# One query unit by way of DRAM, its neighbours spaced anew, and gate stores on GpSimd, in a fused attention and mixture kernel

## The chip, the cores and the metric

The kernel runs on one core of a Trainium2 chip. The engines are named as in the profile: PE (TensorE) multiplies matrices, PEld is its weight load, DVE (VectorE) and ACT (ScalarE) do elementwise work, POOL (GpSimd) does slower elementwise work, SP issues DMAs. The metric is the device time of one execution in microseconds (us); lower is better.

## The reference

Two blocks follow each other. The first is a linear attention with a product feature map, for 4 batches, 4 heads, 1088 tokens and head width 32; the second is a mixture of 4 experts over the 4352 tokens with gates normalised per token, each expert 128 to 1024 to 128.

```python
def phi(x):                                   # S1, S2: 8 x 32
    a = np.einsum('rd,bhsd->bhsr', S1, x)
    b = np.einsum('rd,bhsd->bhsr', S2, x)
    return np.einsum('bhsi,bhsj->bhsij', a, b).reshape(*x.shape[:-1], r * r)
q_p, k_p = phi(q), phi(k)
kv, z = np.einsum('bhsf,bhsd->bhfd', k_p, v), np.sum(k_p, axis=2)
num = np.einsum('bhsf,bhfd->bhsd', q_p, kv)
den = np.einsum('bhsf,bhf->bhs', q_p, z)[..., None] + 1e-06
x = (num / den).transpose(0, 2, 1, 3).reshape(4352, 128)

p = domain_probs / (domain_probs.sum(-1, keepdims=True) + 1e-09)
for e in range(4):
    out += p[:, e:e + 1] * (np.maximum(x @ w1[e], 0.0) @ w2[e])
```

## The kernel before

**The mixture sets the frame.** The tokens are cut into eleven chunks: 128, 448, six of 512, 320, 256 and 128, in the order of the batches. A chunk goes through 16 steps (4 experts, 4 steps each, two blocks of 128 hidden values per step). A half step is one such block: `first` issues its first-layer matmuls, `third` and `lower` finish it, and `behind` issues second-layer matmuls of earlier steps. Chunk 0 and chunk 10 are plain float32 (line 243 in the profile, through `on_side`). Chunk 1 is float32 for experts 0 and 1 (lines 1084 and 1195). All the rest is split into two or three float32r parts: lines 1097, 1098 and 1146 are the first layer, 1214 the second. The splitting of the weights (`weight_parts`, `second_weight_parts`; ACT line 880, DVE line 883) is done at fixed steps during chunks 0 to 2. `ev`, `gate` and `total` (POOL lines 1253 and 1255) weight and sum the experts; `gate` tiles are loaded from the DRAM tensor `gates`, which `store_gates` fills from `pt`.

**The attention is slipped in between.** `start` does the keys of batch 0, its first 128 queries and the projection of the second query unit before chunk 0. What is left is a list, `plan`, of small pieces: (estimated DVE cost, function, name, wait). Each half step of the mixture calls `work`, which adds to a credit, `rate * rooms[...]`, capped at 0.9, and runs pieces while the credit lasts. The rate is what chunks still need over the room that is left until a little ahead of each chunk's start (`EARLY` half steps). A wait such as `("qturn", 2)` holds a piece back until two half steps after the piece of that name. `until_there` forces pieces when a chunk starts. The order so made is fixed when the program is built: each engine then works through its own list in order, and waits where an input is not there.

**Query units.** A batch is cut into three units (`UNITS`). There are two ways for one:

- *Direct* (`queries`, batch 0): transpose the queries (`qT`, line 566), project them on PE with `sq` (line 842), then on DVE two sums and shuffles (lines 845 to 856) lay out both factors, and four half products (line 579) follow.
- *By way of DRAM* (`unit_turn`, `unit_project`, `unit_product`, `unit_visit`; batches 1 to 3): transpose; project on PE with `sx`; ACT copies to `qs` (line 755); SP stores `qs` to `qd` (line 757) and loads it back with repeated rows as `qp` and `qb` (lines 762, 763); DVE makes two full products (line 769).

A *visit* is the PE work against `kvx`, the summed keys of the batch. `attend_inverse`, `attend_scale` and `attend_out` then make the unit's `x` on DVE (`rc`, `xs`, `y`; lines 669 to 695). The second unit of batch 0 is copied by ACT and POOL into the tile `ring` (line 707), from which chunk 1 reads; later units go through the DRAM tensor `xd` into `ring` (lines 713, 722).

**Keys of batches 1 to 3** are 13 pieces each (`key_pieces`: three turns, three projections on line 425 each with its sum, four products), then `key_end` (sums over the tokens on PE, `kvx` on DVE). `load_batch` loads keys and values through SP.

**The lists around the change.** SP's list has, after the weights, 16 gate stores (line 336), two gate loads, then `kn` and `vn` of batch 1. POOL makes `sx` in `later_weights` (line 1014), called at step 8. `sr` is a constant that only `start` reads.

Of the kernel before, what the change touches and what calls it, by code (L numbers as in the profile page):

```python
# [24 lines left out]
def kernel(  # L25
# [30 lines left out]
    R = 8  # L56
# [7 lines left out]
    CW = 512  # L64
    GE = 160
    LA = 2
    LAND, EARLY = 6, 11

    THREE = (0, 1, 3, 4, 5, 6)
    OTHER = [b for b in range(FB) if b not in THREE]  # L70
# [128 lines left out]
        load_w2(e, 1)  # L199
    sk = cpool.tile([P, P], F32, name="sk")  # L200
    sp = apool.tile([32, 3, 2, 32], F32, tag="qf", name="sp")
    sr = cpool.tile([P, 3, 2, P], F32, name="sr")
    sq = cpool.tile([P, P], F32, name="sq")
    sx = cpool.tile([P, P], F32, name="sx")
    nc.gpsimd.memset(sk[:, :], 0.0)
# [122 lines left out]
            out=_ap(pn, 0, P, 0, [[E, G], [1, E]]), in0=dp[:, :, :], in1=_ap(dsum, 0, P, 0, [[1, G], [0, E]]), op=ALU.mult  # L328
        )

    def store_gates():
        nc.vector.transpose(pt[:, :], pn[:, :])
        for b in range(B):
            for e in range(E):
                p = list(pt.ap)[0][0]
                nc.sync.dma_start(
                    gates[b, e].rearrange("(x r j) -> r x j", r=32 // E, j=32),
                    bass.AP(pt.tensor, pt.offset + (32 * b + e) * p, [[E * p, 32 // E], [32, GE // 32], [1, 32]]),
                )
# [178 lines left out]
            for x in range(2):  # L518
                add(0.76, lambda p=p, x=x: key_product(b, 0, NT, p, x, nc.vector), "products")

    def key_end(b, then=None):

        kv = []

        def sums():
            kv.append(held(psum(ps_h, "h")))
            for p in range(2):
                key_sum(b, p, kv[0])
            if then:
                then()  # L530

        def blocked():
            key_blocks(b, kv[0])
            free()

        add(0.1, sums, "keysum", ("products", 3))
        add(0.29, blocked, "keyblocks", ("keysum", 1))
# [31 lines left out]
    def query_turn(b, c, n):  # L569
        qT = apool.tile([P, QW], F32, tag="qT", name="qT")  # L570
        for _ in query_turns(b, c, n, qT):
            pass
        return qT
# [153 lines left out]

    qd = dram.tile([B, len(UNITS[0]), HP, QW], F32, name="qd")

    later = [(b, sum(UNITS[b][:u]), n, u) for b in range(1, B) for u, n in enumerate(UNITS[b])]  # L730
    turned, factors, products, over = {}, {}, {}, {}

    def unit_turn(w):
# [6 lines left out]
    def unit_project(w):  # L740

        b, c, n, u = later[w]
        qT, n2 = turned.pop(w), n // 2
        qc = psum(ps_h, "h")
        for i in range(2):
            for _ in range(2):
                on_side(
                    lambda s: qc[half[s], 0:n2],
                    lambda s: sx[:, HP * i : HP * i + HP],
                    lambda s: qT[:, n2 * s : n2 * s + n2],  # L750
                    start=(i == 0),
                    stop=(i == 1),
                )
        qs = apool.tile([P, QW // 2], F32, tag="qf", name="qs")
        nc.scalar.copy(qs[:, 0:n2], qc[:, 0:n2])
        for s in range(2):
            nc.sync.dma_start(qd[b, u, :, n2 * s : n2 * s + n2], qs[half[s], 0:n2])
        qp = query_tiles()
        qb = [apool.tile([P, QW], F32, tag=t, name="qb") for t in ("qb", "qa")]
        row, at = list(qd[b, u, :, 0:n].ap)[0][0], qd[b, u, :, 0:n].offset  # L760
        for p in range(2):
            nc.sync.dma_start(qp[p][:, 0:n], bass.AP(qd.tensor, at + 16 * p * row, [[row, 16], [0, R], [1, n]]))
            nc.sync.dma_start(qb[p][:, 0:n], bass.AP(qd.tensor, at + (32 + 16 * p) * row, [[0, R], [row, 16], [1, n]]))
        factors[w] = qp, qb

    def unit_product(w, p):
# [15 lines left out]
    def vector_us(n):  # L782

        return 0.16 + n * 1.04e-3
# [3 lines left out]
    def add(cost, run, name, after=None):  # L788

        plan.append((cost, run, name, after))  # L790

    def lay_plan():

        of_first = chain(*(queries(0, c, n) for c, n in ((P, UNITS[0][1]), (P + UNITS[0][1], UNITS[0][2]))))
        for at in range(38):
            add(0.55, lambda: next(of_first, None), "first")
        covers[:] = [(18, P + UNITS[0][1]), (38, S)]
        add(0, lambda: load_rows(q, 1, "qn"), "load")
        key_pieces(1)
        add(vector_us(later[0][2]), lambda: unit_turn(0), "qturn")  # L800
        key_end(1, lambda: unit_project(0))
        for w, (b, c, n, u) in enumerate(later):
            now_on, plan[:] = list(plan), []
            if b + 1 < B:
                if u == 0:
                    key_pieces(b + 1)
                    fill, plan[:] = list(plan), []
                if u == 2:
                    plan[:] = fill
                    key_end(b + 1)  # L810
                else:
                    plan[:], fill = fill[: 5 + u], fill[5 + u :]
            lapse = ("visit" if w else "keysum", LAND)
            for p in range(2):
                add(vector_us(n), lambda w=w, p=p: unit_product(w, p), "product", lapse)
            more = w + 1 < len(later)
            if more:
                add(vector_us(later[w + 1][2]), lambda w=w: unit_turn(w + 1), "qturn")

            def visit(w=w, more=more):  # L820
                if more:
                    unit_project(w + 1)
                unit_visit(w)

            add(0.1, visit, "visit", ("qturn" if more else "product", 2))
            add(0.4, lambda w=w: inverse.__setitem__(w, attend_inverse(*products[w])), "inverse", ("visit", 1))
            add(vector_us(n), lambda w=w: over.__setitem__(w, attend_scale(*products[w], inverse.pop(w))), "scale")
            add(vector_us(n), lambda w=w: unit_out(w), "out")
            plan[:0] = now_on
            covers.append((len(plan), S * b + c + n))  # L830

    covers, inverse = [], {}

    def queries(b, c, n):
        qc = early.pop((b, c), None)
        if qc is None:
            qT = query_turn(b, c, n)
            yield
            yield
            yield  # L840
            qc = held(psum(ps_h, "h"))
            nc.tensor.matmul(qc[:, 0:n], sq[:, :], qT[:, 0:n], start=True, stop=True)
            yield
        qf = apool.tile([P, QW], F32, tag="qf", name="qf")
        nc.vector.stream_shuffle(in_=qc[:, 0:n], out=qf[:, 0:n], mask=mask_lo)
        yield
        nc.vector.tensor_tensor(out=qf[:, 0:n], in0=qc[:, 0:n], in1=qf[:, 0:n], op=ALU.add)
        free()
        yield
        qb = apool.tile([P, QW], F32, tag="qb", name="qb")  # L850
        nc.vector.stream_shuffle(in_=qf[:, 0:n], out=qb[:, 0:n], mask=mask_b)
        yield
        qp = query_tiles()
        for x in range(2):
            qa = apool.tile([P, QW], F32, tag="qa", name="qa")
            nc.vector.stream_shuffle(in_=qf[:, 0:n], out=qa[:, 0:n], mask=mask_a[x])
            yield
            for p in range(2):
                query_product(qp, p, x, n, qa, qb)
                yield  # L860
        yield
        yield
        yield
        yield from attend(b, c, n, qp)
# [142 lines left out]

    def later_weights():

        for h in range(H):
            for to, step, at in ((16 * (h // 2) + h % 2, 2, 0), (32 + R * h, 1, R)):
                nc.gpsimd.tensor_copy(
                    _ap(sx, 32 * h, 32, to, [[HP, 2], [step, R]]), _ap(s_T, 0, 32, at, [[D, 2], [1, R]])
                )
        for h in range(2):
            nc.gpsimd.memset(_ap(by8, 0, P, 32 * h, [[16, 2], [1, 8]]), 1.0 - h)
            nc.gpsimd.memset(_ap(by8, 0, P, 32 * h + 8, [[16, 2], [1, 8]]), 0.0 + h)
        nc.vector.transpose(own8[:, :], by8[:, :])  # L1020
# [246 lines left out]

    start()
    lay_plan()
    place, now, at_of, credit, spent = [0], [0], {}, [0.0], [0.0]  # L1270

    def piece(forced=False):

# [87 lines left out]
    for i in range(len(steps) + LA):  # L1361
        if i < len(steps):
# [11 lines left out]
            def work():  # L1374

                now[0] += 1
                if not NQ <= i < NQ + 2:
                    credit[0] = min(credit[0] + rate * rooms[min(now[0], len(rooms) - 1)], 0.9)
                if holds[0]:
                    credit[0] = max(credit[0], 0.01)  # L1380
                while credit[0] > 0:
                    cost = piece()
                    credit[0] -= cost
                    if not cost:
                        break
# [7 lines left out]
            if i == 2:  # L1393
                gate_quotients()
            elif i == 8:
                later_weights()
            elif i == 5:
                store_gates()
                load_gates(1, range(2))
                load_batch(1)  # L1400
            if m == NC - 2 and kq == NQ // 2:
                until_there(B * S)
                load_last()
# [36 lines left out]
```

## Time and profile before

| | us |
|---|---|
| median of 3 runs | 466.45 (464.6 to 466.86) |
| profiled execution | 466.47 |
| its span, first to last instruction | 464.7 |

| engine | busy us | share of the span |
|---|---|---|
| PE | 452.1 | 97% |
| DVE | 362.5 | 78% |
| ACT | 328.4 | 71% |
| POOL | 110.7 | 24% |

The mean granted clock of PE is 0.996. Chunk 0's matmuls begin at 13.65 us, chunk 1's at 34.85, chunk 1's expert 2 at 62.53, chunk 2 at 84.50, chunk 3 at 138.51.

How to read what follows: a *window* row has the stretch in us from the span's start, its length, the busy us (and instructions) of PE, PEld, DVE, ACT and POOL, the granted clock of PE (1.00 is full), the share of time of the DMA engines and GB/s. A *timeline* row has start, duration, engine, line, operation, out<-in, shape and count; brackets hold the engine's idle time just before and what ended it. The *chain* follows the program back from its last instruction. Matmuls overlap, so a row's duration is longer than the distance to the next one.

### The profile page before, as it was taken

The page shows a single profiled execution, that of the slowest core. Times are in us where ns is not written, and L with a number is a line of the kernel's source. Part 1 is how long each engine was busy: PE and PEld are TensorE (multiplying, and loading weights), DVE is VectorE, ACT ScalarE, POOL GpSimd, SP SyncE. Part 2 cuts the span into 40 slices and gives each one's busy share as a digit, 9 for nine tenths or more (in the row PEclk, how much of TensorE's full clock was granted, in tenths as well). Part 3 has the DMA queues.
Part 4 walks back from the last instruction along what each step waited for, and adds up shares of the span by engine and source line. Part 5 has one row for each costly group of instructions (what it writes and reads, how often), then busy time and mean ns, then how long its engine had stood idle before and what let it go on. Part 6 is the DMA issues. An engine that isn't in the chain of part 4 may idle for free.

```text
span 464.7 us, 8563 instructions
## 1 busy us (share of the span) xinstructions
PE 452.1 (97%) x2991; PEld 350.9 (76%) x2991; DVE 362.5 (78%) x607; ACT 328.4 (71%) x694; POOL 110.7 (24%) x178
## 2 busy tenths in 40 slices
PE   8979999998999999999999999999999999999997
PEld 5765567776777777777777777777777778999987
DVE  5966859798697779787798787787888787878753
ACT  4256568687686678877887776777877786888841
POOL 6320111321332103321233122211221122333120
PEclk9989999999999999999999999999999999999999
DMA  7915060151363314115200340432213210211830
GB/s 221 286 31 129 15 196 20 35 121 37 87 146 119 83 40 108 24 34 137 63 19 27 75 102 14 99 60 86 55 25 99 61 38 16 54 47 31 249 100 18
DMA packets 53171, 37.27 MB, mean 80 GB/s; under 512 B 27304, under 2 KB 47624, under 8 KB 53128
## 3 DMA queue, kind: packets, MB, share of 16 engines
q1 hardware_dynamic: 53112, 36.73, 30.5%
q8 instruction: 23, 0.38, 0.3%
q14 instruction: 20, 0.16, 0.1%
q10 hardware_dynamic: 16, 0.00, 0.0%
HBM read 31.63 MB, written 5.08 MB: 79 GB/s over the span
## 4 chain that ended last, share of the span: by engine, by line
PE 81%; DVE 11%; ACT 3%; DMA 2%; issue 2%; SPq 0%; DVEq 0%; ACTq 0%
PE o L1214 34%; PE h L1146 11%; PE h L1097 10%; PE h L1098 10%; PE h L243 7%; DVE hb L1123 2%; PE o L243 2%; PE h L1084 2%; DVE hd L1126 2%; PE o L1195 2%; PE h L425 1%; DMA kn<-in_k_dram 1%; DMA xd<-y 1%; DVE qp L579 1%; DVE kp L441 1%
## 5 line engine op out<-in xcount | busy, mean ns | idle before, releaser
L1099 ACT ACTIVATE h<-h 128x512 f32<-128x512 f32 (+3 forms) x272 | 146.9, 540 | 80.0 <-PE h L1098 73.8
L1123 DVE SCALAR_TENSOR_TENSOR hb<-h,ha 128x512 fp32r<-128x512 f32 (+3 forms) x204 | 125.8, 625 | 55.8 <-ACT ha L1149 53.8
L1097 PE MATMUL h<-xa,wa 128*128 128x512 f32 (+3 forms) x272 | 125.2, 460 | 0.0
L1126 DVE SCALAR_TENSOR_TENSOR hd<-ha,hb 128x1024 fp32r<-128x1024 f32 (+3 forms) x102 | 117.2, 1149 | 8.5 <-PE h L1098 0.5
L1149 ACT ACTIVATE ha<-h 128x512 fp32r<-128x512 f32 (+3 forms) x204 | 111.7, 547 | 0.0
L1146 PE MATMUL h<-xd,wd 128*128 128x512 f32 (+3 forms) x272 | 103.1, 379 | 0.9 <-ACT h L1099 0.7
L1098 PE MATMUL h<-xb,wb 128*128 128x512 f32 (+3 forms) x272 | 100.4, 369 | 0.0
L1253 POOL TENSOR_TENSOR ev<-ev,gate 128x256 f32<-128x256 f32 (+2 forms) x51 | 41.3, 810 | 233.2 <-DVE ev L1246 213.7
L1214 PE MATMUL o<-ha,vab 128*128 128x512 f32 (+3 forms) x204 | 76.8, 378 | 0.0
L1097 PEld LDWEIGHTS h<-xa,wa 128*128 128x128 f32 x272 | 51.3, 189 | 20.0 <-issue 11.7
L1098 PEld LDWEIGHTS h<-xb,wb 128*128 128x128 f32 x272 | 51.4, 189 | 19.8 <-issue 12.5
L1214 PE MATMUL o<-hid,w_sb 128*128 128x512 f32 (+3 forms) x136 | 63.2, 546 | 0.4 <-DVE ev L1246 0.4
L1146 PEld LDWEIGHTS h<-xd,wd 128*128 128x128 f32 x272 | 51.1, 188 | 13.2 <-ACT h L1099 3.3
L1214 PE MATMUL o<-hd,vd 128*128 128x512 f32 (+3 forms) x204 | 58.9, 370 | 0.0
L1214 PE MATMUL o<-hb,vb 128*128 128x512 f32 (+3 forms) x136 | 50.5, 372 | 0.0
L1255 POOL TENSOR_TENSOR total<-total,ev 128x256 f32<-128x256 f32 (+2 forms) x51 | 45.1, 884 | 4.0
L1214 PEld LDWEIGHTS o<-ha,vab 128*128 128x128 f32 x204 | 38.5, 189 | 6.9 <-issue 0.3
L1214 PEld LDWEIGHTS o<-hd,vd 128*128 128x128 f32 x204 | 36.9, 188 | 6.1
L1154 ACT ACTIVATE hid<-h 128x512 f32<-128x512 f32 (+3 forms) x68 | 37.6, 553 | 0.2 <-PE h L1146 0.2
L1253 POOL TENSOR_TENSOR total<-ev,gate 128x256 f32<-128x256 f32 (+2 forms) x17 | 11.7, 705 | 88.1 <-issue 40.0
L1214 PEld LDWEIGHTS o<-hb,vb 128*128 128x128 f32 x136 | 25.5, 188 | 4.3 <-issue 0.4
L1214 PEld LDWEIGHTS o<-hid,w_sb 128*128 128x128 f32 x136 | 24.5, 188 | 5.1 <-DVE ev L1246 1.0
(142 smaller groups left out, 462.1 us busy)
## 6 DMA issues: line engine op xcount, KB each, us to landing
gate<-gates SPq DMA_DIRECT2D x16, 256.0 KB
kn<-in_k_dram SPq DMA_DIRECT2D x4, 544.0 KB
vn<-in_v_dram SPq DMA_DIRECT2D x16, 128.0 KB
w_sb<-in_moe_w_dram SPq DMA_DIRECT2D x4, 512.0 KB
w_last<-in_moe_w_dram SPq DMA_DIRECT2D x4, 512.0 KB
gate<-gates SPq DMA_DIRECT2D x8, 224.0 KB
qn<-in_q_dram SPq DMA_DIRECT2D x2, 544.0 KB
w_sb<-in_moe_w_dram SPq DMA_DIRECT2D x4, 256.0 KB
```

The costliest lines, as they stand in the source:

```text
L243: nc.tensor.matmul(out(s), weights(s), moving(s), **flags)
L1097: nc.tensor.matmul(g, wa[:, e, w], xa, start=True, stop=False)
L1098: nc.tensor.matmul(g, wb[:, e, w], xb, start=False, stop=True)
L1099: nc.scalar.activation(g, g, ACTF.Copy, scale=1.0 + R12)
L1123: nc.vector.scalar_tensor_tensor(out=hb, in0=g, scalar=0.0, in1=high, op0=ALU.max, op1=ALU.subtract)
L1126: nc.vector.scalar_tensor_tensor(out=d2, in0=a2.bitcast(F32), scalar=R12, in1=b2.bitcast(F32), op0=ALU.mult, op1=ALU.subtract)
L1146: nc.tensor.matmul(g, w, x, start=False, stop=True, skip_group_check=True)
L1149: nc.scalar.activation(ha, g, ACTF.Relu, scale=NEAR)
L1154: nc.scalar.activation(hid[i][j], g, ACTF.Relu)
L1214: nc.tensor.matmul(acc[m, e][o][:, 0:n], w, h, start=first_one, stop=last)
L1253: nc.gpsimd.tensor_tensor(out=to[:, x], in0=ev[:, x], in1=g[:, x], op=ALU.mult)
L1255: nc.gpsimd.tensor_tensor(out=total[m][:, x], in0=total[m][:, x], in1=ev[:, x], op=ALU.add)
```

## The change

- The third unit of batch 0 (512 tokens) goes by way of DRAM like later units. For it a second projection matrix, `first_sx`, is built by POOL in the space of `sr`, with another order of the features, and `qb` is loaded in four pieces per head pair instead of one.
- The pieces get other costs, an order per unit written out by hand (`keys[...]` slices), other waits (products and visits by their own names), the query turn ahead of the products, `EARLY` 14 instead of 11, and a credit cap of 0.5 instead of 0.9.
- `store_gates` is called per batch: batch 0 at step 5 through SP as before, batches 1 to 3 at steps 12, 13 and 14, issued by POOL. So SP's list has 4 gate stores ahead of the gate loads and of `kn` of batch 1, where it had 16.

```diff
-    LAND, EARLY = 6, 11
+    LAND, EARLY = 6, 14
...
-    sr = cpool.tile([P, 3, 2, P], F32, name="sr")
+    sr = cpool.tile([P, 3, 2, P], F32, tag="sr", name="sr")
...
-    def store_gates():
-        nc.vector.transpose(pt[:, :], pn[:, :])
-        for b in range(B):
+    def store_gates(batches):
+        for b in batches:
+            if b == 0:
+                nc.vector.transpose(pt[:, :], pn[:, :])
             for e in range(E):
-                nc.sync.dma_start(
+                (nc.gpsimd if b else nc.sync).dma_start(
...
-    later = [(b, sum(UNITS[b][:u]), n, u) for b in range(1, B) for u, n in enumerate(UNITS[b])]
+    later = [(b, sum(UNITS[b][:u]), n, u) for b in range(B) for u, n in enumerate(UNITS[b]) if b or u == 2]
+    first_sx = {}
...
-                    lambda s: sx[:, HP * i : HP * i + HP],
+                    lambda s: (sx if b else first_sx[0])[:, HP * i : HP * i + HP],
...
+            if b:
+                nc.sync.dma_start(qb[p][:, 0:n], ...)
+                continue
+            for x in range(4):
+                nc.sync.dma_start(
+                    qb[p][32 * x : 32 * x + 32, 0:n],
+                    bass.AP(qd.tensor, at + (32 + 16 * p + R * (x % 2)) * row, [[0, 4], [row, R], [1, n]]),
+                )
...
-        of_first = chain(*(queries(0, c, n) for c, n in ((P, UNITS[0][1]), (P + UNITS[0][1], UNITS[0][2]))))
-        for at in range(38):
-            add(0.55, lambda: next(of_first, None), "first")
-        covers[:] = [(18, P + UNITS[0][1]), (38, S)]
-        add(0, lambda: load_rows(q, 1, "qn"), "load")
-        key_pieces(1)
+        of_first = queries(0, P, UNITS[0][1])
+        costs = [0.62] * 9 + [0.05] * 4 + [0.4, 0.55, 0.6, 0.1, 0.1]
+        for at, cost in enumerate(costs):
+            add(cost, lambda: next(of_first, None), f"first{at}", ("first8", 5) if at == 12 else ("first12", 2) if at == 13 else None)
+        covers.append((len(plan), P + UNITS[0][1]))
         add(vector_us(later[0][2]), lambda: unit_turn(0), "qturn")
-        key_end(1, lambda: unit_project(0))
+        add(0.1, lambda: unit_project(0), "visit", ("qturn", 5))
+        add(0, lambda: None, "wait", ("start", 2 * NQ + 2))
...
+            if b == 0:
+                plan.extend(keys[1][:3])
+            else:
+                at = {(1, 0): (1, 3, 13), (1, 1): (2, 0, 3), (1, 2): (2, 3, 5), (2, 0): (2, 5, 13)}
+                at.update({(2, 1): (3, 0, 3), (2, 2): (3, 3, 9), (3, 0): (3, 9, 13)})
+                if (b, u) in at:
+                    k, z0, z1 = at[b, u]
+                    plan.extend(keys[k][z0:z1])
                 if u == 0:
-                    key_pieces(b + 1)
...
-            lapse = ("visit" if w else "keysum", LAND)
-            for p in range(2):
-                add(vector_us(n), lambda w=w, p=p: unit_product(w, p), "product", lapse)
             more = w + 1 < len(later)
             if more:
                 add(vector_us(later[w + 1][2]), lambda w=w: unit_turn(w + 1), "qturn")
+            for p in range(2):
+                add(vector_us(n), lambda w=w, p=p: unit_product(w, p), "product", ("visit", LAND if w else LAND + 3))
...
-            add(0.1, visit, "visit", ("qturn" if more else "product", 2))
+            add(0.1, visit, "visit", ("product", 3 if w < 4 else 2))
...
-
+        first_sx[0] = cpool.tile([P, P], F32, tag="sr", name="sx0")
+        nc.gpsimd.memset(first_sx[0][:, :], 0.0)
         for h in range(H):
-            for to, step, at in ((16 * (h // 2) + h % 2, 2, 0), (32 + R * h, 1, R)):
+            nc.gpsimd.tensor_copy(
+                _ap(first_sx[0], 32 * h, 32, 16 * (h // 2) + 4 * (h % 2), [[HP, 2], [R, 2], [1, 4]]),
+                _ap(s_T, 0, 32, 0, [[D, 2], [4, 2], [1, 4]]),
+            )
+            for t, to, step, at in (
+                (first_sx[0], 32 + R * h, 1, R), (sx, 16 * (h // 2) + h % 2, 2, 0), (sx, 32 + R * h, 1, R)
+            ):
...
-                    credit[0] = min(credit[0] + rate * rooms[min(now[0], len(rooms) - 1)], 0.9)
+                    credit[0] = min(credit[0] + rate * rooms[min(now[0], len(rooms) - 1)], 0.5)
...
-                store_gates()
+                store_gates(range(1))
                 load_gates(1, range(2))
                 load_batch(1)
+            elif 12 <= i < 12 + B - 1:
+                store_gates(range(i - 11, i - 10))
```

## The prediction

> **What bounds the kernel now.** I read the page's busy table and chain first, then busy time by stage, then the timeline wherever TensorE (PE) was not full. The execution profiled took 466.47 us, its span 464.7, so 1.8 lies outside; the runs' median is 466.45, and sums below start from 466.47.
>
> ```profile
> PE 452.1 (97%) x2991; PEld 350.9 (76%) x2991; DVE 362.5 (78%) x607; ACT 328.4 (71%) x694; POOL 110.7 (24%) x178
> PE 81%; DVE 11%; ACT 3%; DMA 2%; issue 2%; SPq 0%; DVEq 0%; ACTq 0%
> 176.63 3.81 DMA xd<-y
> 170.00:180.00 10.00, 10.00 (x41) 7.48 (x40) 7.34 (x13) 7.15 (x14) 3.77 (x4) 1.00 0.47 116
> ```
>
> The first two lines are the page's busy line and chain: PE is the bound nearly everywhere. The third, from the chain in order of time, looks like a 3.8 us wait for DRAM; the fourth (the window 170 to 180: its length, then busy us of PE, PEld, DVE, ACT, POOL, the granted clock, DMA share, GB/s) shows PE full through it. Nothing is won there. What can be won is where PE stands still or is clocked down.
>
> ```profile
> 3.69:7.11 3.42, 2.13 (x42) 1.40 (x41) 1.97 (x7) 1.37 (x5) 1.49 (x6) 1.00 1.03 238
> 24.17:27.59 3.42, 3.10 (x58) 2.86 (x54) 2.05 (x5) 2.57 (x10) 1.94 (x6) 1.00 0.07 11
> 27.59:31.00 3.41, 1.20 (x4) 0.45 (x6) 1.92 (x5) 1.61 (x5) 0.62 (x3) 1.00 0.05 8
> 31.00:34.41 3.41, 3.41 (x34) 3.41 (x34) 3.00 (x7) 0.38 (x1) 0.00 (x0) 0.50 0.14 37
> 62.53:84.50 21.97, 20.74 (x89) 16.01 (x87) 18.73 (x28) 18.00 (x39) 6.65 (x7) 1.00 0.27 75
> 341.85:353.30 11.45, 11.45 (x72) 8.51 (x72) 9.60 (x13) 8.09 (x16) 2.90 (x4) 1.00 0.10 24
> ```
>
> The same columns. The last row is one expert of a 512-token chunk with nothing else in it: 11.45 us, the floor. In 27.59 to 31.00 PE is busy 1.20 of 3.41 us, and the next stretch of equal length has half the clock.
>
> ```profile
> 26.66 0.61 PE L243 MATMUL h<-x_first,w_sb 128*64 128x128 f32 x8
> 29.80 1.13 PE L842 MATMUL h<-qT,sq 128*128 128x512 f32 x2 [2.53 <-DVE qT L566]
> ...
> 34.85 1.40 PE L1084 MATMUL h<-ring,w_sb 128*128 128x448 f32 x3
> ...
> 48.71 0.69 PE L243 MATMUL h<-kvx,qp 128*64 128x66 f32 x16 [0.88 <-DVE qp L579]
> ...
> 114.53 0.76 PE L243 MATMUL h<-qT,sx 128*64 128x160 f32 x8 [1.25 <-DVE qT L566]
> ```
>
> The timeline of PE, bracketed: idle before, and who ended it. Three stalls: 2.53 us before the third unit's projection, 0.88 before its second head pair, 1.25 before the projection of a later unit.
>
> ```profile
> 24.71 0.67 DVE L695 STREAM_TRANSPOSE y<-xs 128x512 f32<-128x512 f32 x1
> 25.42 2.34 ACT L707 COPY ring<-y 32x128 f32<-32x128 f32 x8 [0.28 <-DVE y L695]
> 19.45 2.03 POOL L1014 COPY sx<-s_T 32x16 f32<-32x16 f32 x8
> 25.45 2.85 POOL L707 COPY ring<-y 32x128 f32<-32x128 f32 x8 [3.65 <-DVE y L695]
> 21.69 11.03 SPq L336 DMA_DIRECT2D gates<-pt x16
> 89.99 1.15 SPq L757 DMA_DIRECT2D qd<-qs  x2
> 92.68 0.58 SPq L762 DMA_DIRECT2D qp<-qd  x1
> ```
>
> Timelines of DVE, ACT, POOL and SP. The 2.34 us of copies into ring stand on ACT ahead of a weight split (27.77) that DVE waits for ahead of that qT. A gate store costs SP 11.03/16 = 0.69 us; from two qd stores to a load of what they wrote it is 2.69 us.
>
> **Part by part. A: chunk 0 and the third unit.** The L842 projection leaves; in the changed order the same unit's projection (four 64x256 matmuls, about 0.95 us) stands behind the last first-layer group of chunk 0, just ahead of chunk 1. The second unit's visit (1.1 us) comes six groups later. PE: from 17.08 thirteen groups at 0.437 us (their pitch in the trace) reach the visit at 22.8, where before it came after seven and waited 0.41. DVE's factors, now behind the 0.9 us of gate sums, are done near 21.9: no wait. Ten groups more: 28.3.
> DVE decides the next point. POOL now makes two matrices: from 19.0 a memset of 0.20 (as for sx), sixteen copies of 0.254 (2.03/8), four small memsets, to 23.5. DVE's own8 transpose waits for that (1.7 us later than before), and behind it stand one split 0.65, one end sum 0.3, a split 0.65, the inverse 0.5, the scaling 0.8, a split 0.65, y 0.67: y ends at 27.7. qT follows at 28.3, when PE asks for it. The projection and one group take PE to 29.7. The ring copies end at 27.7 + 2.85 = 30.55, and chunk 1 starts at 30.6 instead of 34.85: -4.2. PE's idle time near there is some 1 us, so its busy share stays above the 62% (2.13 of 3.42) that kept the full clock, and well above the 35% that did not; 1.7 us (half of 3.41) of the gain is the clock.
> The Trainium skill's page "TensorE: Matmul & The Clock Gate", section "Why this matters for your kernels", asks for no idle gap over about 3 us and tells of a return to half clock after one idle window. By that alone the 2.53 us gap would not have cost the clock, and A would be 1.7 smaller, the total 463.0; the trace has the half clock, so the trace decides.
> Against that: POOL now issues gate stores. Four (batch 1) stand ahead of its ring copies, from 23.5; eight more behind them. Free time is 27.7 - 23.5 = 4.2 us, 1.04 a store. No row shows a store issued by POOL: between 0.12 (its smallest memset) and 2.1 (SP's issue plus half the 2.69 round trip and more, if POOL were held until landing). I take 1.2, SP's 0.69 times 0.73/0.42 (a 128x256 product on POOL against DVE): 4 x 0.16 = +0.6. **A = -3.6**, from -4.2 to +1.7.
>
> **B: the third unit's factors.** Four shuffles (0.73), a sum (0.68) and four half products (0.69) leave DVE, 6.4 us; two full products of 0.68 come in. SP: four stores to 24.5, then gate loads, keys near 27 (33.73 before), values, queries after qT, two qd stores at 31.1, and ten loads of 0.6 from 33.8 to 39.8, landed by 43 if landing takes 3 (kn's first took 4.2). DVE comes to the products near 44.5 and PE to the visit near 50: cover 4 to 5 us, then one for one. The 0.88 us stall goes: **-0.9** (0 if that cover is gone). The later gate stores are wanted past 90 us; keys, nearer, are now loaded 6 us sooner: no cost.
>
> **C: chunk 1's last two experts.** 62.53 to 84.50 is 21.97 us against 2 x 11.45 x 448/512 = 20.0. The key projections of batch 1 (2.1 us of PE) move in here from ahead of it, the next unit's projection (0.95) moves out: PE's sum is unchanged, and is no cost. But ACT, busy 18.00 of 21.97, gets three fs copies and two vx copies, 2.2 us; DVE gets 1.0 and gives back 1.4 (a key product, a qT). Bounds -0.5 and +2.2 (all exposed); **+0.6**, as ACT has 4 us free.
>
> **D: units spaced anew.** Before, qT is the last thing issued ahead of the visit that needs it, two half steps later (a half step is 11.45/8 = 1.43 us). Now it stands ahead of the products, and visits wait three half steps behind those for the early units: the 1.25 us stall at 114.53 goes. **-1.25** (0 if DVE, whose load per expert stays at 9 to 11 of 11.45 us, is late anyway).
>
> **E: due sooner, less saved-up credit.** From 84.5 to 191.8 eight experts cost 8 x 11.45 = 91.6, the attention's own PE pieces 12.5 and switches between matmul kinds about 1.6, together 105.7 of 107.3; D is most of the rest. So sooner due times win nothing: **0**, +-1.
>
> Sum: -3.6 - 0.9 + 0.6 - 1.25 = -5.15, so 461.3.
>
> **Rivals.** (1) POOL holds chunk 1. A store costs 2.1: the ring copies start 4 x (2.1 - 1.04) = 4.2 late, the PE gap passes 4 us, the clock halves (1.7): A = +1.7, 466.6. For it: nothing but the copies feeds ring there. Against: a round trip is a landing time, which SP itself does not wait for between stores.
> (2) Slower: the same place, DVE and POOL getting in each other's way. In the trace a 896-wide hd takes 1.57 us beside a POOL product against 1.09 alone, and a POOL sum 1.46 against 0.74. If each store has to wait out DVE instructions (0.65 each) three times or more, it costs over 2.65, and the total passes 468.8; at 3.5 it is 4 x 2.46 + 1.7 = +11.5 against the -4.2, so 466.47 + 7.3 - 1.55 = 472.2. Against: many DVE instructions there read PSUM or a single tile.
> The Trainium skill's page "SBUF — State Buffer", section "SBUF: two separate sides", gives this rule: DMAs issued by GpSimd need descriptors written by its cores, which DVE instructions in certain modes lock out; it advises the SP or ACT queue. No run here shows it yet.
> (3) The gain is given back in C and the expert behind it: ACT's 2.2 us exposed in both, and D's stall reappearing at an earlier visit: +1.6 + 1.25, about 464.2.
>
> **Numbers.** Forecast 0.62, own range 458.6 (A -4.2, C -0.5, E -1) to 463.5 (C all exposed, 0.6 more on A); (1) 0.14; (2) 0.11; (3) 0.13. The range 458.0 to 467.5 takes in (1) and (3) and leaves out most of (2). A measurement of this kernel tells about 0.5% (2.3 us) from no change: faster (below 464.1) is the forecast and half of (3), 0.68; same 0.20; slower 0.12.
>
> **What would show it.** Right: no half clock behind 4 us; chunk 1's first ring matmul near 31; first L1097 kind of matmul near 57; no PE wait over 1 us at a visit. Wrong: ring copies on POOL that begin over 1 us after y ends (A); products of the third unit waiting for qb to land (B); over 25 us for chunk 1's last two experts (C).

## The result, and the profile after

The changed kernel takes 459.24 us (459.04 to 459.27), the kernel before, run beside it, 466.42 (464.6 to 466.86): a ratio of 0.985, 95% interval 0.983 to 0.988. The forecast was 461.3 in a range of 458.0 to 467.5: the direction held, the gain is 2.1 us larger than forecast. The profiled execution took 459.04, its span 457.3, so the spans differ by 7.4 us. The kernel before's executions fall in two groups: of the 65 measured beside the experiments, 25 took 464.0 to 465.1 us with a mean granted clock of 0.999 or 1.00, and 40, like the profiled one, took 465.8 to 467.8 with 0.993 to 0.996.

The busy line and the chain of the page after:

```profile
PE 450.5 (99%) x2997; PEld 349.9 (77%) x2997; DVE 356.3 (78%) x596; ACT 328.2 (72%) x695; POOL 121.8 (27%) x199
PE 90%; DVE 5%; POOL 2%; issue 1%; DMA 1%; ACT 1%; SPq 0%; DVEq 0%; ACTq 0%
```

PE's busy time fell by only 1.6 us (about the half clock of before); the rest of the 7.4 was idle time. DVE's part of the chain fell from 11% to 5%. The same windows as before around the end of chunk 0, and the stretch of chunk 1's last two experts:

```profile
24.17:27.59 3.42, 3.42 (x68) 3.42 (x64) 3.32 (x11) 1.19 (x4) 1.74 (x4) 1.00 0.57 137
27.59:31.00 3.41, 2.69 (x25) 1.70 (x22) 0.91 (x2) 3.28 (x12) 3.12 (x10) 1.00 0.98 263
55.40:78.93 23.53, 22.48 (x107) 18.03 (x105) 17.97 (x29) 19.29 (x42) 6.13 (x7) 1.00 0.48 125
```

In 27.59 to 31.00 PE is now busy 2.69 of 3.41 us (1.20 before), and the clock stays full up to the end of the work. The DMA share there was 0.05 and is 0.98: the keys', values' and queries' loads of batch 1, free of twelve gate stores, now run here. That number returns below. The timeline of PE:

```profile
22.38 1.13 PE L243 MATMUL h<-kvx,qp 128*64 128x66 f32 x32
...
28.41 1.08 PE L243 MATMUL h<-qT,sx 128*64 128x256 f32 x8 [0.53 <-DVE qT L565]
...
30.12 1.77 PE L1092 MATMUL h<-ring,w_sb 128*128 128x448 f32 x4 [0.19 <-POOL ring L706]
...
49.34 1.11 PE L243 MATMUL h<-kvx,qp 128*64 128x66 f32 x32
```

The second unit's visit (22.38) waits for nothing, the third unit's projection 0.53 us, chunk 1 begins at 30.12 instead of 34.85, and the third unit's visit (49.34) shows no wait. The timelines of POOL, SP and DVE say how near that is to going wrong:

```profile
23.38 2.52 POOL L337 DMA_DIRECT2D gates<-pt  x4
27.59 2.48 POOL L706 COPY ring<-y 32x128 f32<-32x128 f32 x8 [1.68 <-DVE y L694]
30.02 4.61 POOL L337 DMA_DIRECT2D gates<-pt  x8
```
```profile
32.00 2.36 SPq L757 DMA_DIRECT2D qd<-qs  x2
38.39 0.59 SPq L762 DMA_DIRECT2D qp<-qd  x1
```
```profile
45.58 0.69 DVE L776 TENSOR_TENSOR qp<-qp,qb 128x512 f32<-128x512 f32 x1 [1.57 <-DMA qb<-qd]
49.01 0.69 DVE L776 TENSOR_TENSOR qp<-qp,qb 128x512 f32<-128x512 f32 x1 [2.74 <-DMA qb<-qd]
```

A gate store costs POOL 2.52/4 = 0.63 us, and the four are over 1.68 us before `y`. From the first store to `qd` to the first load 6.4 us pass, where the trace of before had 2.69 for a later unit. The second product waits 2.74 us for `qb` and ends at 49.70; PE, whose 32 matmuls begin at 49.34, wants the second half of them some 0.5 us later. The third unit's cover, the time by which its data is ready ahead of PE's demand, is about 0.2 us.

### The profile page after: what moved, and what is told of

Same layout as the page of the kernel before. It is cut to its first block, busy times and chain, and to the rows that moved or that the text cites. A ratio compares the mean times of both kernels' runs of the same rounds, so it can differ in the third digit from the quotient of the medians.

```text
span 457.3 us, 8606 instructions
## 1 busy us (share of the span) xinstructions
PE 450.5 (99%) x2997; PEld 349.9 (77%) x2997; DVE 356.3 (78%) x596; ACT 328.2 (72%) x695; POOL 121.8 (27%) x199
## 3 DMA queue, kind: packets, MB, share of 16 engines
q1 hardware_dynamic: 53272, 37.85, 31.1%
## 4 chain that ended last, share of the span: by engine, by line
PE 90%; DVE 5%; POOL 2%; issue 1%; DMA 1%; ACT 1%; SPq 0%; DVEq 0%; ACTq 0%
PE o L1222 38%; PE h L1154 12%; PE h L1105 12%; PE h L1106 12%; PE h L243 7%; PE h L1092 3%; PE o L1203 3%; PE o L243 2%; PE h L426 1%; DMA kn<-in_k_dram 1%; DVE hb L1131 1%; POOL sx L1022 1%; POOL ring L706 0%; DVE hd L1134 0%; DVE kp L442 0%
## 5 line engine op out<-in xcount | busy, mean ns | idle before, releaser
L1261 POOL TENSOR_TENSOR ev<-ev,gate 128x256 f32<-128x256 f32 (+2 forms) x51 | 39.5, 774 | 229.5 <-DVE ev L1254 207.3
L1263 POOL TENSOR_TENSOR total<-total,ev 128x256 f32<-128x256 f32 (+2 forms) x51 | 49.0, 960 | 4.0
```

The costliest lines, as they stand in the source:

```text
L1261: nc.gpsimd.tensor_tensor(out=to[:, x], in0=ev[:, x], in1=g[:, x], op=ALU.mult)
L1263: nc.gpsimd.tensor_tensor(out=total[m][:, x], in0=total[m][:, x], in1=ev[:, x], op=ALU.add)
```

## The experiments

Each was compared with runs of the kernel before on the same chip, at 465.9 to 466.2 us. The changed kernel was not run again beside them: its 459.24 (ratio 0.985) is from its own comparison, and the medians of the kernel before differ by up to 0.5 us between comparisons. The labels `b_` are edits to the kernel before, `a_` to the changed one.

**What chunk 0's end is worth: the clock, the stall.** `b_warm`:

```diff
+            for _ in range(10):
+                nc.tensor.matmul(qc[:, :], warm[:, 0:P], warm[:, :], start=True, stop=True)
```

ahead of the third unit's projection: PE works through the 2.53 us gap, and nothing else changes.

> The kernel before, with ten dummy bf16 matmuls (128x512, 0.21 us each at full clock) put on PE just ahead of the third unit's projection, into the bank that it then overwrites: PE is kept busy in the 2.53 us gap and nothing else moves. If the half clock after 31 us comes from that gap, 1.7 us (half of 3.41) go: 464.7 against 466.4. If the half clock has another cause, or a gap shorter than a whole 3.4 us window does not matter: 466.4 or more.

Measured 464.67 (464.24 to 465.42), ratio 0.998 (0.9966 to 0.9993). The window behind the gap, of `b_warm`:

```profile
31.00:34.41 3.41, 3.41 (x42) 2.46 (x38) 3.37 (x9) 1.83 (x5) 0.00 (x0) 1.00 0.14 40
```

Its clock, 0.50 before, is 1.00, and all twelve executions have a mean of 0.999 or 1.00. Filling the gap with idle work alone returns 1.5 us against the 1.7 counted for it. `b_projlate` moves the same projection to just ahead of chunk 1 instead, which takes the stall away too:

```diff
-            add(0.55, lambda: next(of_first, None), "first")
+            add(0.55, lambda: next(of_first, None), "turned" if at == 18 else "first", ("turned", 8) if at == 21 else None)
```

> The kernel before with one wait more in the list of pieces: the third unit's projection (its direct way is kept) comes just ahead of chunk 1, where the changed kernel has its projection, instead of 6 half-layer groups earlier. If the stall and the half clock in chunk 0 are most of the gain, PE now waits some 1.4 us there (for a hidden tile behind ACT's ring copies) instead of 2.53, at full clock, and chunk 1 starts near 32 instead of 34.85; DVE's factors come later, so the visit's stall stays or grows: 463.4 to 464.4. If the gain needs the way by DRAM, the wait only moves to the visit: 466.

Measured 463.83 (463.69 to 464.1), ratio 0.9961 (0.9947 to 0.9975). Chunk 1 begins at 32.29 (34.85): 2.6 us of the 4.7 that the change wins there come from moving one projection.

**The gate stores.** `b_gates` is the kernel before with `store_gates` cut up and issued as in the change, nothing else; `a_gates_sp` is the changed kernel with all 16 stores on SP as before:

```diff
-                (nc.gpsimd if b else nc.sync).dma_start(
+                nc.sync.dma_start(
...
-                store_gates(range(1))
+                store_gates()
```

> The kernel before with the gate part of the change alone: batch 0 stored by SP, batches 1 to 3 by POOL at steps 12 to 14, so SP reaches the keys' load some 8 us sooner. By my account nothing on PE's path waits for keys or gates there: 466.4 within 0.5. If the earlier keys carry the gain: 463.5 or less.

> The changed kernel without its gate part: all 16 gate stores on SP ahead of gate loads, keys, and the third unit's trip through DRAM. 12 stores of 0.69 are 8.3 us more on SP. In the changed trace DVE already waited 1.57 and 2.74 us for qb to land and had no slack left, so I expect the products 4 to 8 us later and PE waiting at the visit: 463 to 466. If SP has that time to spare: 459.2.

`b_gates`: 466.29, ratio 1.0006 (0.9991 to 1.0021), nothing. `a_gates_sp`: 469.19 (467.1 to 470.47), ratio 1.0065 (1.0041 to 1.0088): slower than the kernel before, a miss by 3 us or more. Its waits of PE, and one window:

```profile
PE h L243 <- DVE qp L775: 5.2, 2, 2.9
...
54.52:64.76 10.24, 7.34 (x39) 4.43 (x40) 7.27 (x16) 2.08 (x4) 0.00 (x0) 0.50 0.24 65
```

With twelve more stores ahead of it on SP, `kn` is issued at 34.46 instead of 25.52; DVE stands 9.1 us for it at the turn of the keys, the third unit's trip starts 10 us later, both halves of its visit stall (5.2 us), and the clock is halved for 10.24 us, in which PE is busy 7.34, so that it costs half of that, 3.7. The 5.2, the 3.7 and 2.0 for a `hid` sum to 10.9, against a span 11.4 longer. So the gate part wins nothing alone and is worth 10 us beside the third unit's trip.

**POOL as the place that holds chunk 1.** `a_pool12` puts all twelve POOL stores ahead of the ring copies:

```diff
-            elif 12 <= i < 12 + B - 1:
-                store_gates(range(i - 11, i - 10))
+            elif i == 12:
+                store_gates(range(1, B))
```

> The changed kernel with all twelve POOL gate stores at step 12, so that eight more stand ahead of POOL's ring copies. A store took 0.63 us in the changed trace, so POOL is free at 23.4 + 12 x 0.62 = 30.8 instead of 25.9, and the ring copies start 3.2 us after y. By rival 1's mechanism chunk 1 starts 3.2 us later, and PE's gap of about 3.7 us halves the clock for 3.41 us (1.7 more): 464.1. Without the clock's share: 462.4. If PE does not wait for POOL's half of the copies: 459.2.

Measured 464.89 (461.27 to 467.91), ratio 0.999 (0.9961 to 1.0019). Its waits of PE:

```profile
PE h L1092 <- POOL ring L706: 3.5, 1, 3.5
```

The mechanism of rival (1) is real: eight more stores, 5 us, push the ring copies past `y`, and behind a gap of 3.5 us the clock is halved as well (0.50 from 32.71 to 36.12, PE busy 3.02, so 1.5 us more). Between POOL's 23.38 and `y` at 27.5 six stores of 0.63 us fit; the change has four there.

`a_own8first` makes `own8` ahead of the two projection matrices on POOL, which takes away DVE's 0.80 us wait for it:

```diff
+        for h in range(2):
+            nc.gpsimd.memset(_ap(by8, 0, P, 32 * h, [[16, 2], [1, 8]]), 1.0 - h)
+            nc.gpsimd.memset(_ap(by8, 0, P, 32 * h + 8, [[16, 2], [1, 8]]), 0.0 + h)
+        nc.vector.transpose(own8[:, :], by8[:, :])
...
-        for h in range(2):
-            nc.gpsimd.memset(_ap(by8, 0, P, 32 * h, [[16, 2], [1, 8]]), 1.0 - h)
-            nc.gpsimd.memset(_ap(by8, 0, P, 32 * h + 8, [[16, 2], [1, 8]]), 0.0 + h)
-        nc.vector.transpose(own8[:, :], by8[:, :])
```

> The changed kernel with POOL's four by8 memsets and the own8 transpose behind them put ahead of the two projection matrices. In the changed trace DVE stood 0.80 us for by8 and PE 0.53 for qT and 0.19 for the ring copies behind that: at most 0.7 us to win, 458.6. If another wait is behind it at once (ACT's hidden tiles, the weight split): 459.2.

Measured 458.58 (458.46 to 460.52), ratio 0.9868 (0.9844 to 0.9892); chunk 1 begins at 29.73 (30.12). Two of its six executions took 460.3 and 460.5, at full clock; why is open. Its ratio to the kernel before is no better than the changed kernel's 0.985, so the times do not show that it is faster.

**Order and pace.** `a_oldorder` restores the order of a unit's last steps, `a_oldpace` the due times and the cap:

```diff
-            if more:
-                add(vector_us(later[w + 1][2]), lambda w=w: unit_turn(w + 1), "qturn")
...
+            if more:
+                add(vector_us(later[w + 1][2]), lambda w=w: unit_turn(w + 1), "qturn")
-            add(0.1, visit, "visit", ("product", 3 if w < 4 else 2))
+            add(0.1, visit, "visit", ("qturn" if more else "product", 2))
```
```diff
-    LAND, EARLY = 6, 14
+    LAND, EARLY = 6, 11
...
-                    credit[0] = min(credit[0] + rate * rooms[min(now[0], len(rooms) - 1)], 0.5)
+                    credit[0] = min(credit[0] + rate * rooms[min(now[0], len(rooms) - 1)], 0.9)
```

> The changed kernel with the old order within a unit: products, then the next unit's query turn, then the visit two half steps after the turn. By part D the stall for qT comes back at one or more visits, 1.25 us in all: 460.5. If the order within a unit is not what took that stall away: 459.2.

> The changed kernel with EARLY 11 and the credit cap 0.9 as before. By part E the pace wins nothing by itself: 459.2 within 0.6. If sooner due times or the smaller cap carry a share of the gain, it is over 460.2.

Both missed. `a_oldorder`: 465.99 (464.2 to 467.25), ratio 1.0006 (0.9989 to 1.0022), all of the gain gone. Its timeline:

```profile
49.29 0.69 DVE L776 TENSOR_TENSOR qp<-qp,qb 128x512 f32<-128x512 f32 x1 [2.74 <-DMA qb<-qd]
...
51.98 0.70 DVE L565 STREAM_TRANSPOSE qT<-qn 128x512 f32<-128x512 f32 x1
...
52.73 1.97 PE L243 MATMUL h<-qT,sx 128*64 128x256 f32 x8 [4.52 <-DVE qT L565]
```

The next unit's `qT` now stands on DVE behind a product that waits 2.74 us for `qb` and behind four weight splits, and PE, which needs `qT` ahead of the visit, stands 4.52 us; the clock is 0.50 for the 6.83 us from 50.28, in which PE is busy 4.37, which costs 2.2 more. Together that is the 6.7 us by which the span is longer; chunk 2 begins 6.3 us later than in the changed kernel (85.27 and 78.93). `a_oldpace`: 462.43 (460.47 to 466.68), ratio 0.9952 (0.9922 to 0.9982); one row of its PE timeline:

```profile
50.01 0.69 PE L243 MATMUL h<-kvx,qp 128*64 128x66 f32 x16 [2.72 <-DVE qp L776]
```

The visit is asked for at 46.60 instead of 49.34, the trip ends where it did (its second product begins at 49.26), and the difference is a stall. The run undoes `EARLY` and the cap together, so which of the two moves that date is not told apart.

**One place or many?** `a_oldorder_w1` uses the old order for all units but the third one of batch 0 (`if more and w` at the turn, the new wait for `w` = 0).

> The changed kernel with the old order of a unit's last steps (products, then qT, visit two half steps behind qT) for every unit but the third one of batch 0, which keeps the new order. If a_oldorder's 6.8 us were all lost at the third unit's visit, where qT stood behind products that waited 2.74 us for qb: 459.0 to 459.8 us, no PE wait above 1.3 us at a later visit. By the prediction's step D, the order is worth 1.25 us at later units: 460.5. Rival, the order decides at every unit: 462 or more.

Measured 460.02 (459.02 to 460.49), ratio 0.9873 (0.985 to 0.9895): 6.0 of the 6.8 us lost by `a_oldorder` were lost at the third unit's visit. Of what is left, its profile shows 0.85 us at that visit again (the trip's second product begins at 49.61, where the changed kernel has 49.01). Waits of PE for a later unit's `qT` sum to 0.5 us (0.2 and 0.3): the order decides little there.

**What stretches the trip?** `a_qnlate` issues batch 1's query load (544 KB) behind the two `qd` stores instead of ahead of them; `a_oldpace_qnlate` adds the old pace:

```diff
-        if u == len(UNITS[b]) - 1 and b + 1 < B:
+        if b and u == len(UNITS[b]) - 1 and b + 1 < B:
             load_rows(q, b + 1, "qn")
...
             nc.sync.dma_start(qd[b, u, :, n2 * s : n2 * s + n2], qs[half[s], 0:n2])
+        if b == 0:
+            load_rows(q, 1, "qn")
```

> The changed kernel with the query load of the next batch (544 KB) issued after the third unit's two stores to DRAM instead of before them. If the bulk loads stretch the round trip: the load of qp is issued near 35.5 to 36 instead of 38.4, the products of the third unit wait under 0.5 us for qb instead of 2.74; the time stays 459.2 +- 0.4, since PE did not wait for them. Rival, the queries then come late for the next batch's first unit: 460 or more.

> The changed kernel with the old due times and credit cap (a_oldpace, 462.43) and the same query load behind the stores. If the old pace cost its 3.2 us only because PE asks for the third unit some 1.8 us sooner than its trip through DRAM ends: the stall of 2.72 us goes, 459.3 to 460. Rival, the pace is worth its 3 us spread over later units: 462.0 to 462.5.

`a_qnlate`: 458.9 (458.82 to 458.99), ratio 0.985 (0.983 to 0.987); the time is as expected, the trip is not. SP's timeline:

```profile
30.79 4.03 SPq L757 DMA_DIRECT2D qd<-qs  x2
34.92 0.53 SPq L109 DMA_DIRECT2D qn<-in_q_dram  x1
38.03 0.58 SPq L764 DMA_DIRECT2D qp<-qd  x1
```

The first store goes out 1.2 us sooner, the second is held until 34.3 although both halves of `qs` come from one copy that ended at 30.8, and the load still waits until 38.03 (38.39). So the query load is not what holds it. SP's own waits name what does, the first two lines from the changed kernel, the last two from `a_qnlate`:

```profile
SPq L757 <- DMA kn<-in_k_dram: 1.8, 1, 1.8
SPq L757 <- DMA vn<-in_v_dram: 1.3, 1, 1.3
...
SPq L757 <- DMA kn<-in_k_dram: 3.0, 1, 3.0
SPq L757 <- DMA gate<-gates: 1.4, 1, 1.4
```

Each store waits for the transfer eight places ahead of it in SP's list to land: `kn` and the first `vn` in the changed kernel, the second gate load and `kn` in `a_qnlate`, where the query load no longer stands between. The instructions in the traces show why: SP's transfers signal on eight semaphores in turn, and one waits for the last transfer on its own. `kn` (544 KB) was issued at 25.52 and 25.64 and let its store go at 32.00 and 34.3, at a DMA share of 0.9 to 1.1. So the loads of keys and values hold the stores; no run moved them out of the way. The rest is the second store's landing: from its issue to the load it is 4.5 us in the changed kernel, 3.7 in `a_qnlate` and 3.5 in `a_gates_sp`, which has no POOL stores there, against 2.1 for the later unit in the trace of before. How the loads and POOL's eight stores share in that stays open.

`a_oldpace_qnlate`: 460.99 (460.18 to 462.32), ratio 0.9899 (0.9878 to 0.9919), between the two expectations: as the trip is not shorter, the stall is still there, 2.28 us. It agrees with the pace mattering through that one date; it does not show it as cleanly as meant.

**The two edits joined.** `a_best` joins `own8` first and the late query load:

> The changed kernel with the own8 matrix made ahead of the projection matrices (a_own8first, 458.58, with some executions at 460.3) and the query load behind the stores. If the executions at 460.3 come from the third unit's trip that ends with no cover: 458.3 to 458.7 and none above 459.2. Rival, they come from the clock elsewhere: the same median, still some at 460.3.

Measured 458.43 (457.99 to 459.03), ratio 0.9841 (0.9819 to 0.9862): the lowest median, some 8 us under the kernel before. None of its four executions is above 459.2, as expected if those at 460.3 came from the trip, but four are few to tell by. Its interval overlaps the changed kernel's (0.983 to 0.988), so that it is faster than that is not shown, and its range overlaps those of both its parts.

## Why the prediction was right, and where its sum was off

The sum of the prediction against the trace. Starts of the same work are compared, and PE work that the change moved across the point (key projections, 2.1 us out ahead of chunk 1's expert 2 and 1.9 ahead of chunk 3; a projection, 0.95 in) is put back:

| step | forecast us | trace us | from |
|---|---|---|---|
| A | -3.6 | -4.7 | chunk 1: 34.85 to 30.12 |
| B | -0.9 | -1.25 | expert 2 of chunk 1: 62.53 to 55.40, + 2.1 - 0.95, less A |
| C | +0.6 | -0.2 | expert 1 of chunk 2: 98.89 to 92.74 |
| D | -1.25 | -1.5 | chunk 3: 138.51 to 128.96, + 1.9 |
| E | 0 | +0.25 | the end: 464.7 to 457.3 |
| sum | -5.15 | -7.4 | |

**A: right in each date, one term mis-sized.** Forecast and trace: the visit 22.8 and 22.38, POOL free at 23.5 and 23.38, `y` done at 27.7 and 27.5, `qT` 28.3 and 28.26, the ring copies' end 30.55 and 30.07. The term that failed is the POOL store: 1.2 us was taken, between 0.12 and 2.1, and it measures 0.63, nearest to SP's 0.69. Scaling it by how much slower POOL does elementwise work was the error: issuing is not that kind of work. The 0.6 us that it added did not arise; the other 0.5 is `y`, 0.2 sooner, and ring copies of 2.48 us where 2.85 was taken. `b_warm` bears out the clock's part, which the kernel before pays in 40 of 65 executions.

**B: the sign right, the cover wrong.** This is the step that failed. "From two qd stores to a load of what they wrote it is 2.69 us" was read where the DMA engines were little used, and applied where the same change brings three bulk loads: the loads start at 38.39, not 33.8, and the last lands 4 us after its issue, at 49.0, not 43. Of the 4.6 us at the start, some 2.2 are SP's wait for `kn` and `vn` to land (the second store goes out at 33.9, where 31.1 and 0.6 for the first make 31.7), and 2.4 the store's longer way. The cover is 0.2 us, not 4 to 5, and the sign of being wrong that the prediction named for B came: both products wait for `qb`, 1.57 and 2.74 us. That the gain came all the same is luck, the margin of a date, and the order, the pace and the gate part each turn it into a stall of 2.3 to 5 us when undone.

**C:** the 0.6 us for ACT's added copies did not show; ACT is busy 19.29 of 23.53 us. The working took the next unit's projection out of 62.53 to 84.50, but in the trace of before it stands behind that, at 88.51; counted up to chunk 2's expert 1, PE's sum is unchanged, as it said.

**D and E: the sums near, the reasons not.** The 1.25 us stall for a later unit's `qT` is gone, but not by the order within a unit alone: with the old order at later units the waits for `qT` sum to 0.5 us. With the old pace and the new order there is none at a later unit either. Both of these runs keep the order of pieces between units that the change writes out by hand (the key slices); it was not undone alone, so that it removes the stall is left as likely, not shown. And "sooner due times win nothing" is wrong for this kernel: undone together with the cap, they cost 3.2 us, 2.7 of it a stall at one visit of batch 0 that E's window (84.5 to 191.8) did not include. The way by DRAM itself was not taken out of the changed kernel alone, so its own share of the gain is not known; `b_projlate`, without it, wins 2.3 us.

**The rivals.** (1) is refuted by 0.63 us and shown as a mechanism by `a_pool12`. (2) is refuted: in 24.17 to 27.59, with DVE busy 3.32 of 3.42 us, POOL's stores up to 25.90 take 0.63 us each, and DVE's splits beside them 0.65 to 0.69 as elsewhere. The Trainium skill's page "SBUF — State Buffer", section "SBUF: two separate sides", warns that DVE can lock GpSimd out of writing descriptors. At this place no issue is held; the stores land late (a median of 5.3 us from issue), and whether a lock-out or the busy DMA engines (0.89 from 26 to 28) delay them no run here tells. PE does not wait for them. (3) did not come: chunk 1's end gave back nothing.

## What to carry to other kernels

Price a round trip through DRAM in the stretch in which it will run, with what else the change puts on the DMA engines, and write the cover as two dates, the landing and the demand. Where the cover is near zero, edits of order and pace that look neutral decide the time, and parts can't be priced one by one: the gate part alone was worth nothing, and taking it out of the whole cost 10 us. A PE gap is paid twice when the clock goes with it, so a stall's price is its length, plus half of what PE is busy in the halved stretch behind it.

## What the runs showed of the hardware

- A gap's length alone did not decide the clock. Before, 2.53 us of idle PE was followed by 3.41 us at 0.50; in `a_oldpace` 2.72 us (PE busy 0.69 of the 3.41 us from 46.60) was followed by a full clock. What did was PE's busy time in fixed windows of 3.41 us. In each trace the clock changes on whole multiples of 3.413 us from the first entry of its record: in the trace of before 3.69 and 31.00 (eight), in `a_oldorder` 5.91 and 50.28 (thirteen), in `a_gates_sp` 6.74 and 54.52 (fourteen). Two such windows, of `a_oldorder` (its gap halved the clock) and `a_oldpace` (its gap did not):

```profile
46.87:50.28 3.41, 1.34 (x4) 0.38 (x2) 0.99 (x3) 0.48 (x1) 1.27 (x2) 1.00 0.33 86
...
45.67:49.08 3.41, 1.62 (x24) 0.94 (x24) 0.69 (x1) 1.47 (x4) 0.00 (x0) 1.00 0.37 120
```

- In all fourteen traces, up to the end of the work, every window of this grid in which PE was busy 1.34 us or less (there are seven) is followed by one at half clock, and no full-clock window in which it was busy 1.62 us or more is. A halved window with 2.77 us of busy PE was followed by another, one with 3.02 by a full clock. The first entry lies between 3.60 and 6.74 us, so the same gap falls differently into the windows from execution to execution, which fits the two groups of the kernel before. The Trainium skill's page "TensorE: Matmul & The Clock Gate", section "What's actually happening", tells of an activity window of 3.4 us that runs freely. The traces agree: the halved stretches of 3.41, 6.83 and 10.24 us are one, two and three windows.
- A gate store of 5 KB costs the issuing engine 0.58 to 0.63 us on POOL and 0.64 to 0.71 on SP.
- SP is held by its own earlier transfers: in `a_qnlate` the second of two stores, its data ready, went out 3.5 us after the first, when `kn`, eight places ahead, had landed; in the later units the two take 1.15 us together.
